# Left output rows in an accumulator of their own, and memory rows transposed by 128 columns, in a recurrent-memory attention kernel

## The chip, the cores and the metric

The kernel runs on one core of a Trainium2 chip. The metric is the device time of one execution in microseconds (us). The kernel before was timed three times: median 1837.84 us, from 1831.92 to 1839.93. Besides, one execution was taken by the hardware profiler.

## The reference

The output is the sum of three terms over x of 2048 tokens by 1024: x itself, a memory-augmented attention over the normalised x, and a feed-forward block with tanh-GELU on the same. The attention goes through the tokens in 64 segments of 32, one after the other, because each takes eight memory rows from the one before:

```
for s in range(n_seg):                       # 64 segments of 32 tokens
    h = concatenate([mem, xs])               # 8 memory rows + 32 tokens
    q, k, v = h @ Wq, h @ Wk, h @ Wv         # 32 heads of 128
    p = softmax(where(mask, q k^T * scale, -1e9))
    o = (p v) @ Wo
    mem = o[:8]; outs.append(o[8:])          # the memory rows feed the next segment
```

Weights are bfloat16, 1024 x 4096 for each of Wq, Wk, Wv and 4096 x 1024 for Wo: 32 MB in all, more than fits on the core.

## The kernel before

*Stages.* Until about 450 us the kernel does the layer norm and the feed-forward block (lines 304 to 643). Its result with x added, R, is kept in DRAM (`R_n`) and laid out anew for the recurrence by `turn_R` (L433): as rows of the main tokens in `hr_d` and of the left tokens in `hrL_d`. From then on come the 64 segments.

*Main and left rows.* A segment's own pass has only 32 rows: 24 tokens and 8 memory rows. The last 8 tokens of each segment, called left, are put together for four segments (32 rows) and have their Q, K, V and output made at a later time. Which is made in which segment goes by the kind of the segment, `i4 = s % 4` (L730 to L733): left K first half in kind 3 and second in kind 0, left Q first half in kind 1 and second in kind 2, left V first in kind 0 and second in kind 3, and the left output in kind 1 (and in the last segment). `og` and `slot` number the group and the place in it.

*Weights.* They are cut into 64 units of 128 x 2048: 8 for each of six half passes in the order K0, Q0, K1, Q1, V0, V1, and 16 for the output pass, O. 46 stay in SBUF. 18 are streamed anew in each segment through a ring of six buffers: SP issues the load of the next one as soon as PE has used up a buffer (`unit_done`, `start_stream`). In O, units 3, 6, 8, 11, 14 and 15 are streamed. Two of the 18 are kept in PSUM and copied to the ring by VectorE (DVE) at L245, two copies of 128 x 512 words each; the one that is unit 4 of Q0 is copied right after the first unit of K0. One more is kept in SBUF by five eighths.

*One product.* PE's array is used in four column strips of 32. A unit's `product` (L738) is four matmuls of 128 x 32 weights (the activations, loaded) by 512 columns, one for each strip. Products of left rows use the same unit with other activations (`hL`) into an accumulator of their own. There are three accumulators in PSUM (`acc`), one bank for scores and small things (`mixed`), and four with kept weights.

*The output pass* (L1109 to L1123). `o_product(n, t, acc)` multiplies unit n, two heads. In kinds 0, 2 and 3 the first nine units put even and odd heads into different strips, so that after unit 9 `fold` (L1001) adds the two halves on ScalarE (ACT) and DVE, and the other seven go to a second accumulator. In kind 1 main and left rows go through one accumulator of 64 columns' width in two halves, with no fold. `values(1, ...)` (L926), the attention's second half of heads, is made inside this pass after unit 5; its results are copied out of PSUM by ACT and DVE and are the weights of units 8 to 15.

*The turn* (L1124 to L1161). The new memory rows have to reach the next segment's `hT`, the transposed input. They are copied or added out of the accumulator to `o_sb` (by ACT at L1130 in kind 1, by DVE with the folded half at L1134 in the others), `put_mem` (L286) transposes them with matmuls against unit columns, and DVE casts them into `hr_home` (L297). Up to six left products of the next segment are "led" (`lead_products`, L753): three ahead of `put_mem` and three after it. Then the residual R is added (L1154) and the rows are stored: in kinds 0, 2, 3 by four DMAs on POOL (L1188); in kind 1 by four DMAs (two on ACT, two on POOL, L1160) to `outL_d` in DRAM, and from there to the output (L1185).

*Queues.* ACT, DVE, POOL and SP work in the order of the program. POOL carries the load of the next segment's x and R (`hr_home`, L267), the load of the left residual (`pd_main`, L1121), most stores, and in segments 1 to 5 the `small` DMAs of `turn_R`, which are put in one or two at a time after streamed units. The order of all work is written out by hand; the framework adds the waits.

Of the kernel before, what the change touches and what calls it, by code (L numbers as in the profile page):

```python
# [17 lines left out]
P = 128  # L18
S = 2048
DM = 1024  # L20
# [36 lines left out]
AT_BANKS, AT_PART = 5, 4  # L57
PART_COLS = 1280
# [31 lines left out]
def kernel(  # L90
# [37 lines left out]
    outL_d = dram.tile([NGRP, 2 * SEG, DM], BF16, name="outL_d")  # L128
# [157 lines left out]
    def put_mem(o_sb, hT, ps, nb=4):  # L286
# [4 lines left out]
        for c in range(nc_):  # L291
            for q in range(4):
                nc.tensor.matmul(  # L293
                    psM[32 * q:32 * q + 32, c, :, :], lhsT=o_sb[:, 4 * c + q, :], rhs=rows,
                    start=(c == 0), stop=True, skip_group_check=True, tile_position=(0, 32 * q),
                )
# [7 lines left out]
    with tc.tile_pool(name="ma", bufs=2) as ma, tc.tile_pool(name="mps", bufs=6, space=PSUM) as mps:  # L304
# [124 lines left out]
        def with_left(seg):  # L429

            return seg % GRP == 1 or seg == NSEG - 1

        def turn_R(ttg, eng, small=None):  # L433
# [3 lines left out]
            for i in range(4):  # L437
# [3 lines left out]
                both = [  # L441
                    t[:, 256:512].rearrange("(h r) c -> r h c", h=2)
                    for t in (hr_d[min(4 * og + 1, NSEG - 1) + 1, :, :], hrL_d[og, :, :])
                ]
                halves = [rows.rearrange("t (h w) c -> t w h c", w=2)[:, w, :, :] for w in range(2)]
                if with_left(seg):
                    m0 = SEG
                    pairs = [(both[w][m0:m0 + SEG, :, :], halves[w]) for w in range(2)]
                else:
                    pairs = [(hr_d[seg + 1, :, 256:512].rearrange("(j t) c -> t j c", j=4), rows)]  # L450
# [5 lines left out]
                for r0 in rows_at:  # L456
                    pairs += [(both[w][r0:r0 + NL, :, :], halves[w][NX:SEG, :, :]) for w in range(2)]
# [62 lines left out]
        for tg in range(4):  # L520
# [88 lines left out]
            else:  # L609
# [4 lines left out]
                put_mem(o_sb, nxt["hT"], mps.tile([P, 512], F32, name="ps"))  # L614
# [35 lines left out]
    with tc.tile_pool(name="late", bufs=1) as late, \  # L650
# [69 lines left out]
        for s in range(NSEG):  # L720
# [14 lines left out]
            m0 = SEG if left_o else main_row(slot)  # L735
            st = {}

# [188 lines left out]
            def values(u, rs):  # L926
# [18 lines left out]
                for r in rs:  # L945
# [4 lines left out]
                    else:  # L950
                        parts = [
                            ((outL if u else outs0)[:, h, NL * slot:NL * slot + NL], 0, NL),
                            (outM[:, h, :] if u else outs0[:, h, m0:m0 + SEG], NL, 40),
# [17 lines left out]
            def o_product(n, t, acc):  # L971
# [3 lines left out]
                w, i, u = unit  # L975
                for k in range(2):
                    h = 4 * (i % 4) + 2 * u + k
                    main = outM[:, h, :] if i >= 4 else outs0[:, h, m0:m0 + SEG]
                    if left_o:
                        lhs = [(0, 32, outL[:, h, :]), (32, 32, main)] if i >= 4 else [(0, 64, outs0[:, h, :])]  # L980
                        tiles = [(64 * r + r0, w, (2 * r, 2 * r + 1), lhsT) for r0, w, lhsT in lhs for r in range(2)]
                        start, stop = n == 0 and k == 0, n == 15 and k == 1
                    elif n < NPAIR:
                        tiles = [(64 * k + 32 * r, 32, (r, r + 2), main) for r in range(2)]
                        start, stop = n == 0, n == NPAIR - 1
                    else:
                        tiles = [(32 * r, 32, (r,), main) for r in range(4)]
                        start, stop = n == NPAIR and k == 0, n == 15 and k == 1
# [116 lines left out]
            at = {5: [lambda: values(1, (0, 1))]}  # L1105
# [3 lines left out]
            psX = new_acc()  # L1109
            for n, unit in enumerate(O_UNITS):  # L1110
                t = unit_tile(unit)
                if n == NPAIR and not left_o:
                    st["folded"] = fold(psX)
                    psX = new_acc()
                o_product(n, t, psX)
                unit_done(unit)
                for fn in at.get(n, ()):
                    fn()
                if n == 6 and left_o:
# [4 lines left out]
            nw = 2 if left_o else 1  # L1124
            if not final:
                o_sb = outM
                no = 16 if left_o else 8
                o = psX[:, 0:32 * no].rearrange("p (h e) -> p h e", e=32)
# [97 lines left out]
```

## Time and profile before

| | |
|---|---|
| median of three runs | 1837.84 us |
| the profiled execution | 1834.89 us |
| its span, first to last instruction | 1833.2 us |
| granted TensorE clock | 0.998 |
| PE busy / DVE / ACT / POOL | 94% / 52% / 36% / 15% |
| DRAM traffic over the span | 336 GB/s |
| first segment begins at | 363.5 us |
| a group of four segments, 605 to 1740 us | 85.2 to 88.6 us |

On the profile's page each digit of a row is the busy share of one of 40 equal slices, in tenths. A group's line names the source line, the engine, the operation, what is written and read, shapes, count, then busy time, mean length of one, and the idle time ahead with what ended it. A window's row gives the length, busy time and count for PE, PE's weight loads, DVE, ACT and POOL, the granted clock, and the share and rate of the 16 DMA engines. Matmuls overlap, so that four of 380 ns in four strips start within some 10 ns and the next four 215 ns later. The landing of SP's own transfers is not in the trace.

### The profile page before, as it was taken

The numbers are of one execution on the slowest core, as the hardware profiler recorded it, in microseconds if no ns is written. First come the engines' busy times: TensorE is split into PE (matmuls) and PEld (weight loads), VectorE is DVE, ScalarE is ACT, GpSimd is POOL, SyncE is SP. The second block draws the span as 40 slices with busy tenths as digits, with TensorE's granted clock in tenths as the row PEclk, the third lists the DMA queues.
The fourth block names the chain that finished last, engine by engine and source line by source line (L and its number), as shares of the span: only waits on it lengthen the run. The fifth ranks groups of instructions, "written<-read, shape, count | busy, mean of one in ns | idle before, by whom it ended". The sixth has DMA issues, their size and how long they took to land.

```text
span 1833.2 us, 71272 instructions
## 1 busy us (share of the span) xinstructions
PE 1720.8 (94%) x31117; PEld 872.6 (48%) x31137; DVE 962.2 (52%) x2444; ACT 665.4 (36%) x1509; POOL 276.4 (15%) x542
## 2 busy tenths in 40 slices
PE   8999999998998999999999999999999999999997
PEld 4444444444444444554445545444445444444444
DVE  7657483805554545545455555555555454545543
ACT  6334251602333333333333334333333333333333
POOL 0000001500342111112111111111111111111111
PEclk9999999999999999999999999999999999999999
DMA  9921212769999999999999999999999999999997
GB/s 291 319 85 46 55 44 57 261 209 367 400 398 365 383 389 390 380 385 380 376 382 389 393 385 386 389 387 391 374 389 383 373 393 383 381 380 390 378 386 301
DMA packets 230821, 604.65 MB, mean 330 GB/s; under 512 B 46795, under 2 KB 86267, under 8 KB 230508
## 3 DMA queue, kind: packets, MB, share of 16 engines
q1 hardware_dynamic: 207252, 579.67, 83.6%
q0 software_dynamic: 16384, 16.64, 2.9%
q8 instruction: 244, 4.00, 0.9%
q10 hardware_dynamic: 6872, 3.78, 0.7%
q14 instruction: 69, 0.57, 0.1%
HBM read 586.02 MB, written 29.10 MB: 336 GB/s over the span
## 4 chain that ended last, share of the span: by engine, by line
PE 42%; DMA 22%; issue 3%; DVE 2%; ACT 1%; DVEq 0%; ACTq 0%; SPq 0%; POOLq 0%
PE acc L744 29%; DMA u<-Wc_V 10%; PE acc L991 9%; DMA u<-Wc_O 7%; DMA u<-Wc_Q 2%; DMA u<-Wc_K 2%; PE acc L934 1%; DVE d_oL L1012 1%; DVE u L245 1%; DMA hr_home<-hr_d 1%; PE mixed L853 1%; ACT mixed L897 1%; PE mixed L293 1%; PE mixed L859 0%; ACT q_all L1130 0%
## 5 line engine op out<-in xcount | busy, mean ns | idle before, releaser
L744 PE MATMUL acc<-u,hr_home 128*32 128x512 bf16 x11520 | 790.3, 380 | 43.7 <-DMA u<-Wc_V 17.5
L744 PEld LDWEIGHTS <-hr_home 128*32 128x32 bf16 x12288 | 334.1, 96 | 352.0 <-issue 60.2
L744 PE MATMUL acc<-u,hrL 128*32 128x512 bf16 x2880 | 247.2, 379 | 2.1 <-issue 1.0
L473 PE MATMUL ps<-u 128*128 128x512 bf16 (+1 forms) x920 | 194.4, 373 | 2.0 <-ACT u L390 2.0
L245 DVE TENSOR_SCALAR u<-kept 128x512 uint32<-128x512 uint32 x254 | 163.6, 686 | 62.0 <-PE acc L991 41.6
L795 ACT CAST d_oL<-acc 128x512 bf16<-128x512 f32 x128 | 74.6, 583 | 275.0 <-PE acc L744 275.0
L991 PE MATMUL acc<-u,q_all 128*32 128x256 bf16 (+1 forms) x2207 | 133.8, 300 | 20.0 <-DMA u<-Wc_O 15.0
L594 PE MATMUL ps<-u 128*128 128x512 bf16 x657 | 146.2, 379 | 0.8
L473 PEld LDWEIGHTS <-u 128*128 128x128 bf16 x920 | 89.8, 98 | 104.9 <-issue 2.4
L1188 POOL DMA_DIRECT2D out_dram<-hr_home x188 | 96.3, 513 | 260.8 <-DVE hr_home L1154 247.0
L991 PE MATMUL acc<-u,d_oL 128*32 128x512 bf16 (+1 forms) x1536 | 131.6, 382 | 1.2 <-DMA u<-Wc_O 0.7
L907 DVE TENSOR_TENSOR pd_main<-half_home,mixed 128x320 bf16<-128x320 bf16 x128 | 62.4, 488 | 132.2 <-ACT mixed L897 132.2
L809 DVE STREAM_TRANSPOSE q_all<-q_all 128x512 bf16<-128x512 bf16 x128 | 90.6, 708 | 71.1 <-ACT q_all L795 71.0
L991 PEld LDWEIGHTS <-q_all 128*32 128x32 bf16 x3381 | 99.8, 96 | 58.9 <-issue 27.9
L799 ACT CAST q_all<-acc 128x512 bf16<-128x512 f32 x128 | 75.2, 587 | 139.1 <-PE mixed L859 138.7
L267 POOL DMA_DIRECT2D hr_home<-hr_d x58 | 32.8, 565 | 591.0 <-PE acc L744 572.6
L744 PEld LDWEIGHTS <-hrL 128*32 128x32 bf16 x3072 | 84.9, 96 | 51.3 <-issue 7.6
L795 ACT CAST q_all<-acc 128x512 bf16<-128x512 f32 x128 | 75.2, 587 | 93.5 <-PE acc L744 93.5
L594 PEld LDWEIGHTS <-u 128*128 128x128 bf16 x672 | 65.3, 98 | 77.3 <-DVE g_u L555 0.4
L897 ACT ACTIVATE mixed<-mixed,small_consts 128x160 f32<-128x160 f32 x256 | 94.3, 368 | 8.4
L547 ACT ACTIVATE g_xb<-ps,b1col 128x512 bf16<-128x512 f32 x112 | 76.8, 686 | 55.5 <-PE ps L473 54.7
L991 PEld LDWEIGHTS <-d_oL 128*32 128x32 bf16 (+1 forms) x2048 | 65.5, 99 | 59.1 <-issue 12.2
(137 smaller groups left out, 2104.6 us busy)
## 6 DMA issues: line engine op xcount, KB each, us to landing
u<-Wc_K SPq DMA_DIRECT2D x256, 512.0 KB
u<-Wc_V SPq DMA_DIRECT2D x256, 512.0 KB
u<-Wc_O SPq DMA_DIRECT2D x256, 512.0 KB
u<-Wc_Q SPq DMA_DIRECT2D x192, 512.0 KB
u<-in_B_w_dram SPq DMA_DIRECT2D x28, 512.0 KB
u<-Wc_O SPq DMA_DIRECT2D x64, 192.0 KB
hr_home<-hr_d POOLq DMA_DIRECT2D x58, 128.0 KB, 5.3
u<-in_A_Wq_dram SPq DMA_DIRECT2D x13, 512.0 KB
```

What stands on the lines that cost most here:

```text
L245: nc.vector.tensor_single_scalar(out=out, in_=in_, scalar=0, op=ALU.bitwise_or)
L473: nc.tensor.matmul(ps[:, SEG * s0:SEG * s1].rearrange("p (s t) -> p s t", t=SEG), lhsT=w1_sb[fb // 2][:, kt, (fb % 2) * P:(fb % 2 + 1) * P ...
L547: nc.scalar.activation(out=xb[:, :], in_=ps[:, :], func=ACT.Identity, bias=b1col[:, fb:fb + 1], scale=1.0)
L594: nc.tensor.matmul(ps[:, :], lhsT=gts[fc // 4][:, fc % 4, t * P:(t + 1) * P], rhs=w2_sb[fc // 2][:, fc % 2, cs], start=(fc == 0), stop=(fc ...
L744: nc.tensor.matmul(o, lhsT=lhs[:, i, :], rhs=m, start=(i == seq[0]), stop=(i == seq[-1]), tile_position=(0, 32 * j),)
L795: cp(out=out, in_=ps.rearrange("p (h e) -> p h e", e=32))
L799: cp(out=t[:, :], in_=ps[:, :])
L809: nc.vector.transpose(out=home, in_=home)
L897: nc.scalar.activation(out=mixed[:, 160 * b:160 * b + 160], in_=mixed[:, 0:160], func=ACT.Exp, scale=-1.0, bias=off[:, b:b + 1],)
L907: nc.vector.tensor_tensor(out=pdA.rearrange("p c b q -> p b c q"), in0=prA[:, None, :, :].to_broadcast([P, 2, 4, 40]), in1=dd, op=ALU.mult,)
L991: nc.tensor.matmul(acc[r0:r0 + rows, c:c + wide], lhsT=lhsT, skip_group_check=True, rhs=cols, start=start, stop=stop, tile_position=(0, r0),)
L1188: nc.gpsimd.dma_start(out=out_flat[rows, 256 * j:256 * j + 256], in_=res[32 * j:32 * j + NX, :])
```

## The change

Lines of the kernel after are shown with +.

1. `put_mem` takes four heads at once as 128 columns: two matmuls where there were 8 (16 in kind 1). Only the very first call keeps the old form.
2. In kind 1 (and the last segment) the main rows go through O as in the other kinds, with the fold after unit 12. The left rows get an accumulator of their own, `psL`: for ten units their product follows the main one, and for units 0, 1, 2, 4, 5 and 7 it is put off: three ahead of `put_mem` and three after it.
3. In kind 1 no left Q products are led; the second left Q half is made wholly in the pass Q1 of kind 2.
4. `values(1)` in kind 1 is made in two halves, after unit 5 and after unit 7; the first eight heads' results go to `pr_all`. The left residual's load comes after unit 7 in place of 6.
5. Main rows of kind 1 are stored straight from `hr_home`, as in the other kinds. The left rows are added to their residual in four steps and stored by one DMA on ACT; `outL_d` and the residual rows in `hrL_d` have a layout by four column blocks, so that `turn_R` needs one DMA for a piece of left rows where it took two.

```diff
+LEFT_LATER, LEFT_PAIR = (0, 1, 2, 4, 5, 7), 12
...
-    def put_mem(o_sb, hT, ps, nb=4):
+    def put_mem(o_sb, hT, ps, nb=4, wide=True):
...
         for c in range(nc_):
+            if wide:
+                nc.tensor.matmul(
+                    psM[:, c, :, :], lhsT=o_sb[:, 4 * c:4 * c + 4, :].rearrange("p h e -> p (h e)"), rhs=rows,
+                    start=(c == 0), stop=True, skip_group_check=True,
+                )
+                continue
             for q in range(4):
...
-                if with_left(seg):
-                    m0 = SEG
-                    pairs = [(both[w][m0:m0 + SEG, :, :], halves[w]) for w in range(2)]
-                else:
-                    pairs = [(hr_d[seg + 1, :, 256:512].rearrange("(j t) c -> t j c", j=4), rows)]
+                pairs = [(hr_d[seg + 1, :, 256:512].rearrange("(j t) c -> t j c", j=4), rows)]
...
-                for r0 in rows_at:
-                    pairs += [(both[w][r0:r0 + NL, :, :], halves[w][NX:SEG, :, :]) for w in range(2)]
+                left = hrL_d[og, :, 256:512].rearrange("(j t) c -> t j c", j=4)
+                pairs += [(left[r0:r0 + NL, :, :], rows[NX:SEG, :, :]) for r0 in rows_at]
...
-            m0 = SEG if left_o else main_row(slot)
+            m0 = main_row(slot)
+            low_outs = pr_all.rearrange("p (h t) -> p h t", h=8) if left_o else outM[:, 0:8, :]
...
+            def o_product(n, t, acc, left=0):
+                pairs = LEFT_PAIR if left_o else NPAIR
                 for k in range(2):
                     h = 4 * (i % 4) + 2 * u + k
+                    if left:
+                        lhs = outL[:, h, :] if i >= 4 else outs0[:, h, 0:SEG]
+                        tiles = [(64 * k + 32 * r, 32, (r, r + 2), lhs) for r in range(2)]
+                        start, stop = left == 1, left == 16
...
-            at = {5: [lambda: values(1, (0, 1))]}
+            if left_o:
+                at = {5: [lambda: values(1, (0,))], 7: [lambda: values(1, (1,))]}
+            else:
+                at = {5: [lambda: values(1, (0, 1))]}
...
+            def left_product(n, t):
+                nonlocal left_made, psL
+                if psL is None:
+                    psL = new_acc()
+                left_made += 1
+                o_product(n, t, psL, left_made)
+
             for n, unit in enumerate(O_UNITS):
                 t = unit_tile(unit)
-                if n == NPAIR and not left_o:
+                if n == (LEFT_PAIR if left_o else NPAIR):
                     st["folded"] = fold(psX)
                     psX = new_acc()
                 o_product(n, t, psX)
+                if left_o and n in LEFT_LATER:
+                    left_later.append((n, t))
+                elif left_o:
+                    left_product(n, t)
                 unit_done(unit)
...
-                if left_o:
-                    nc.scalar.copy(out=o_sb[:, 0:no, :], in_=o)
...
-                if (i4 == 3 or more) and not final:
+                if i4 != 1 and (i4 == 3 or more):
...
                     lead_products(LEAD // 2)
-                put_mem(o_sb, nxt["hT"], mixed[:, 224:288], 4 // nw)
+                for _ in range(len(left_later) // 2):
+                    left_product(*left_later.popleft())
+                put_mem(o_sb, nxt["hT"], mixed[:, 224:288])
                 if led:
                     lead_products(LEAD)
+            while left_later:
+                left_product(*left_later.popleft())
...
+            nc.vector.tensor_tensor(out=res, in0=flat, in1=res, op=ALU.add)
+            if left_o:
+                resL = st["resL"]
+                for k in range(2):
+                    for b in range(2):
+                        q = slice(64 * b, 64 * b + 64)
+                        nc.vector.tensor_tensor(
+                            out=resL[q, :], in0=psL[64 * k:64 * k + 64, 256 * b:256 * b + 256], in1=resL[q, :],
+                            op=ALU.add,
+                        )
+                let_go(psL)
+                if not final:
+                    nc.scalar.dma_start(out=outL_d[og, :, :], in_=resL)
```

## The prediction

> **What bounds the kernel now.** I read the page first (parts 1 to 3), then windows over single stages, then the waits of TensorE, then the timeline of one turn. All sums are made against the profiled execution, 1834.89 us (span 1833.2), which stands 2.95 us below the median of the runs, 1837.84.
>
> The page's busy shares, DMA row and first queue:
>
> ```profile
> span 1833.2 us, 71272 instructions
> ...
> PE 1720.8 (94%) x31117; PEld 872.6 (48%) x31137; DVE 962.2 (52%) x2444; ACT 665.4 (36%) x1509; POOL 276.4 (15%) x542
> ...
> DMA  9921212769999999999999999999999999999997
> ...
> q1 hardware_dynamic: 207252, 579.67, 83.6%
> ```
>
> PE looks like the bound at 94%, but from slice 11 on the 16 DMA engines are at 9 as well, nearly all of it the weight stream of queue q1. Windows over the end of segment 25 and the start of 26 (columns: us, busy time by engine, clock, DMA share, GB/s) tell where each leads:
>
> ```profile
> 990.45:994.45 4.00, 4.00 (x52) 1.94 (x48) 1.24 (x4) 1.98 (x6) 0.96 (x2) 1.00 1.03 404
> 994.45:997.00 2.55, 2.55 (x50) 1.34 (x52) 1.29 (x2) 0.00 (x0) 0.16 (x1) 1.00 1.04 398
> 997.00:1000.00 3.00, 2.91 (x74) 1.39 (x66) 0.45 (x2) 0.58 (x1) 0.00 (x0) 1.00 0.84 315
> 1000.00:1003.00 3.00, 3.00 (x64) 1.52 (x56) 2.54 (x6) 0.58 (x1) 1.12 (x2) 1.00 1.02 357
> 1003.00:1010.00 7.00, 7.00 (x200) 3.99 (x192) 4.18 (x13) 3.19 (x8) 2.44 (x5) 1.00 1.03 396
> ```
>
> A share of 1.03 is DMA at its limit; only about the turn of a kind-1 segment it falls to 0.84. There the six stream buffers are full and SP waits for PE. From the 13 groups of four segments at 605 to 1740 us: mean 87.26 us, DMA share 1.003. At 1.03 the same traffic takes 87.26 x 1.003 / 1.03 = 85.0 us, so 2.3 us of each group is lost DMA time. Over the same four-microsecond stretch (6 to 10 us after the output pass begins) the 13 windows average a share of 0.86, that is 0.68 us lost, and with its two neighbours 0.9 us.
>
> A rule that speaks the other way: the Trainium skill (Perfetto Trace Analysis, Roofline) puts the ceiling of a core's 16 DMA engines at about 435 GB/s. A group moves 385 GB/s x 87.26 us = 33.6 MB, by the rule 77 us: ten us of slack, PE alone the bound, and earlier buffers worth nothing. The rows never exceed 410 GB/s where the share is 1.03, so I take 85.0. The groups themselves agree: summing PE's gaps over 150 ns by what ended them, those not ended by a DMA range from 0.95 to 4.16 us a group, and the group's length doesn't follow them (correlation -0.01; beside the group's DMA time as second variable, 0.24 us per us). PE stalls are paid out of PE's own waits for the stream, 2.4 us a group:
>
> ```profile
> PE acc L744 <- DMA u<-Wc_V: 17.5, 38, 1.8
> PE acc L991 <- DMA u<-Wc_O: 15.8, 33, 1.5
> ```
>
> **The change part by part.** Times are from the start of the output pass (O) of a kind-1 segment, 990.45 in segment 25. Before, O takes 16 units of 0.43 us: attention values at 2.71, last product over at 7.5, first K product of the next segment at 9.17, the same in 10 of 16 such segments.
>
> *O pass.* Six left products (each 4 matmuls, 0.215 us) leave: -1.29. But `values(1)` now comes after six units that take 5 x 0.215 + 0.43 = 1.5 us, while its probabilities (L912) end at 1.76 to 1.87: kinds 0 and 2, whose O is already single, finish it at 2.12. I take 2.05 for its first half, a stall of about 0.35. In two halves, each with the same 0.245 us (both row tiles ran side by side), it costs +0.25, and the second half needs the first's bank, which ACT empties 0.72 us after the first half (2.77): +0.1 with the drain. Then eight units of 0.44: O ends at 6.75, **0.75 earlier**. `fold` at unit 12 has four double units (1.7 us) against 2.05 that it takes in single segments; three left products (0.645) cover the rest.
>
> *Turn.* The timeline before:
>
> ```profile
> 998.23 0.58 ACT L1130 CAST q_all<-acc 128x512 bf16<-128x512 f32 x1 [4.10 <-PE acc L991]
> 998.86 0.27 PE L293 MATMUL mixed<-ident_mem,q_all 128*32 128x16 bf16 x16
> 999.21 0.23 DVE L297 CAST hr_home<-mixed 128x64 bf16<-128x64 f32 x1 [2.76 <-PE mixed L293]
> 999.62 0.39 PE L744 MATMUL acc<-u,hr_home 128*32 128x512 bf16 x4
> 999.78 0.42 DVE L1154 TENSOR_TENSOR pd_main<-acc,pd_main 128x256 bf16<-128x256 f32 x1 [0.34 <-DMA pd_main<-hrL_d]
> 1000.12 0.42 DVE L1154 TENSOR_TENSOR hr_home<-acc,hr_home 128x256 bf16<-128x256 f32 x1
> 1000.45 1.28 DVE L245 TENSOR_SCALAR u<-kept 128x512 uint32<-128x512 uint32 x2
> ```
>
> Six products fill it before and after (led Q before, left output after), ACT's 0.58 becomes DVE's add of 0.42, over at 7.47; memory product 7.53 to 7.70 (below), three left products, K begins at 8.34, **0.83 earlier**.
>
> *What is late next.* DVE's queue: after the memory copy and the residual add stand now four adds of 64 partitions (0.34 apart, the last two waiting on the first two) in place of two, behind the landing of the left residual, and behind them the two copies L245 that PE needs at its 13th product (Q unit 4). The residual's DMA is issued at 3.78 (3.60 before; it follows the values), and lands a median of 4.9 us later:
>
> ```profile
> DMA to landing us min/median/max: 2.5/4.9/5.8
> ```
>
> With 5.1 (the mean of the steady ones): adds from 8.98, copies from 10.45 to 11.73. PE reaches that product at 8.34 + 2.59 = 10.93: **a new stall of 0.85**, which eats K's lead. ACT's store of the left rows waits for the same adds, and ACT's copy of K behind it; DVE's transpose comes later still, so it adds nothing.
>
> *Second Q pass of kind 2.* Six more products, +1.29; the 0.28 that PE waits there for `keep_q` (L883 on L245) goes. Sum for PE in a group: -0.83 + 0.85 + 1.29 - 0.28 = **+1.03**. The waits for the stream hide it: at 0.24 it is +0.25 a group, in 15 groups +3.7 (with that cover gone, +15).
>
> *DMA.* O's six streamed units and the first three of the next segment give their buffers back 0.65 to 0.85 earlier, exactly where DMA is idle (0.9 to be had): -0.7 a group, **-10.5**. Traffic: 128 packets of 512 B less into `outL_d`, main rows straight from SBUF, left rows in smaller packets; at 27 ns for 512 B and 46 for 1024, over 16 engines, 0.13 us a group: -2.
>
> *Memory rows by 128 columns*, all 64 turns. The 8 matmuls took 0.064 us of PE (16: 0.114). Phase A's 128-column loads stand 0.056 apart, so two take 0.11. The Trainium skill (TensorEngine Tiling, Tiling Modes) says that a change of tiling mode drains the array, and these are the only 128x128 ones here. The row agrees:
>
> ```profile
> 993.40 0.18 PE L940 MATMUL acc<-q_all,VL 64*128 64x32 bf16 x2
> ...
> 993.51 0.62 PE L991 MATMUL acc<-u,d_oL 128*64 128x512 bf16 x4
> ```
>
> 0.10 from one mode to the other. So 0.17, +0.1 a turn by the rule, +0.05 without; I take 0.1, in full at the 16 turns after kind 3 (PE leads there, DMA at 0.88 to 0.95), at 0.24 at 32 others: +2.4. If no transition cost shows it is half.
>
> *Start.* Turning R into rows takes one DMA in place of two for each left piece: 34 on POOL in segments 1 to 4 in place of 57. Before, that backlog reaches segment 5:
>
> ```profile
> 550.06 2.08 POOL L1188 DMA_DIRECT2D out_dram<-hr_home  x4 [3.23 <-issue]
> 558.02 0.58 POOL L267 DMA_DIRECT2D hr_home<-hr_d  x1 [5.88 <-PE acc L991]
> ```
>
> Segment 4's stores go out at 550, 13 us into segment 5, and the load of x behind them lands 6 us late; segment 5 takes 26.4 us against 23. The stream catches up a part: -2.5. *End*: 1.29 of left products and four adds after the last output, partly beside the first add: +0.5.
>
> Sum: -10.5 + 3.7 - 2 + 2.4 - 2.5 + 0.5 = **-8.4 us**; 1837.84 - 8.4 = 1829.4.
>
> **Rivals.** *DMA binds wholly* (0.20): PE's additions vanish in its waits, and the rows' 0.24 is noise. For it: the zero correlation. Against: four of 13 groups have under 1.5 us of DMA waits. -10.5 - 2 - 2.5 + 1.6 (the turns after kind 3): 1824.
>
> *The earlier buffers win nothing* (0.16): the six products merely change places with the led ones, the turn still gives no buffer back for 1.7 us (1.9 before), and the hole moves along. Then -2 - 2.5 + 2.4 + 0.5: 1836. For it: the hole lies in the turn, not in O. Against: in the steady trace it has a left edge, 6 us into O, where the backlog ends.
>
> *Slower* (0.20): the left residual lands late because DMA is now full in that window. Place: DVE's adds ahead of L245, in kinds 1 to 2. Each us of landing beyond 5.1 is one more us of PE stall; the 2.4 us of waits that pay for it are gone when it reaches 5.1 + 2.4 - 1.03 = 6.5, and the gain is used up near 7. At 8 us: +1.5 x 15 over the cover, less 10: **1850**. For it: loads of x at full DMA reach 6.8. Against: the longest of this one is 5.8.
>
> **How the numbers follow.** The likeliest case (0.44) gives 1829.4, with its own range 1821 to 1838 from: gain on DMA 0.45 to 0.9 a group (7 us), PE counted at 0 to 0.5 (7 us), 128-column turns 0.05 to 0.15. 0.5%, 9.2 us, is about what a measurement of this kernel can tell from no change (the three runs span 8). Faster by over 0.5%: a half of the likeliest and all of the first rival, 0.42; within: the other half and the third, 0.38; slower 0.20. The range 1817 to 1846 leaves out a part of the slow case and the fast tail.
>
> **What would show it.** O's span in kind 1 falls from 7.5 to 6.75 with a PE wait ahead of the values; DMA share at 6 to 10 us rises from 0.86 towards 0.95; PE waits at L744 on DVE's copy in the second segment of each group, 0.85; PE's waits for the stream shrink below 2.4 a group; segment 5 is 23 us. Wrong if the share in the hole stays, or if PE's waits for DVE exceed 2 us a group.

## The result, and the profile after

The changed kernel takes 1842.8 us (median of 20 runs, 1836.4 to 1850.7) against 1836.4 us for the kernel before (20 runs, 1828.5 to 1843.2). The ratio is 1.0033 with a 95% interval of 1.0019 to 1.0046: slower by 6 us, where 8.4 us faster was forecast. 1842.8 lies inside the range of 1817 to 1846; the direction was wrong.

The page of the changed kernel, whose profiled span is 1838.7 us:

```profile
span 1838.7 us, 71935 instructions
...
PE 1728.9 (94%) x31410; PEld 891.5 (48%) x31430; DVE 1005.5 (55%) x2545; ACT 668.1 (36%) x1526; POOL 264.0 (14%) x515
...
q1 hardware_dynamic: 206852, 579.66, 83.8%
```

PE is busy for 8 us more. The windows over the same stretches of segment 25 and 26 as before, counted from the start of the output pass (columns: us, busy time by engine, clock, DMA share, GB/s):

```profile
992.67:996.67 4.00, 3.87 (x76) 1.90 (x72) 1.25 (x5) 2.02 (x6) 0.71 (x2) 1.00 1.03 404
996.67:999.22 2.55, 2.55 (x69) 1.75 (x65) 1.96 (x4) 0.74 (x2) 0.41 (x1) 1.00 1.04 404
999.22:1002.22 3.00, 3.00 (x62) 1.43 (x58) 1.78 (x6) 0.00 (x0) 0.81 (x2) 1.00 0.98 363
1002.22:1005.22 3.00, 2.15 (x44) 0.99 (x36) 2.88 (x6) 0.58 (x1) 1.23 (x3) 1.00 1.01 350
1005.22:1012.22 7.00, 7.00 (x171) 4.19 (x164) 3.35 (x12) 2.96 (x7) 2.21 (x4) 1.00 1.01 390
```

The third row is the hole that the change was to close: its DMA share went from 0.84 to 0.98. Over the same stretch of all 13 groups (6 to 10 us into the output pass) the mean share rose from 0.86 to 0.95. The fourth has the new stall: PE is busy for 2.15 of 3.00 us. The timeline of that turn (start, length, engine, line, then the idle time ahead and what ended it):

```profile
1001.47 1.78 DVE L1170 TENSOR_TENSOR pd_main<-acc,pd_main 64x256 bf16<-64x256 f32 x4 [0.51 <-PE acc L739]
1003.28 1.29 DVE L246 TENSOR_SCALAR u<-kept 128x512 uint32<-128x512 uint32 x2
```

```profile
1002.09 1.68 PE L739 MATMUL acc<-u,hr_home 128*32 128x512 bf16 x28
1004.62 0.61 PE L739 MATMUL acc<-u,hr_home 128*32 128x512 bf16 x8 [0.85 <-DVE u L246]
```

The first K product starts at 1001.01, 8.34 us into O as forecast (8.34 to 8.36 in five of the 13 groups; in the others a wait inside O makes it later, median 8.59 against 9.17 before). DVE makes the four left sums, then the two copies of kept weights, and PE waits 0.85 us for them. Over the whole kernel, the waits of PE (us in total, times, longest):

```profile
PE acc L739 <- DVE u L246: 15.0, 16, 1.4
PE acc L739 <- issue: 10.9, 16, 1.9
PE acc L739 <- DMA u<-Wc_V: 10.5, 24, 1.8
...
PE acc L990 <- DMA u<-Wc_O: 7.2, 15, 1.2
```

The waits for the stream shrank (`Wc_V` 17.5 to 10.5, `Wc_O` 15.8 to 7.2), and 15 us of waits for DVE came. Mean lengths of a segment over the 13 groups from segment 8 to 59:

| us | kind 0 | kind 1 | kind 2 | kind 3 | group |
|---|---|---|---|---|---|
| before | 21.76 | 23.10 | 20.76 | 21.64 | 87.26 |
| after | 21.73 | 22.32 | 21.73 | 21.73 | 87.51 |

Kind 1 gained 0.78 us and kind 2 lost 0.97. What DMA won in kind 1 it lost in kind 2: its mean rate went from 386 to 396 GB/s in kind 1 and from 381 to 368 in kind 2. The same stretch late in kind 2, 12 to 16 us after segment 26 begins, kernel before and then after:

```profile
1011.43:1015.43 4.00, 2.89 (x63) 1.47 (x67) 0.74 (x3) 1.57 (x5) 0.56 (x1) 1.00 1.03 411
```

```profile
1012.68:1016.68 4.00, 4.00 (x120) 2.08 (x108) 2.09 (x6) 2.52 (x7) 0.58 (x1) 1.00 0.95 337
```

Before, PE had time to spare there (2.89 of 4.00) and the DMA share was 1.03; after, PE has none and DMA falls to 0.95 (means over 13 groups: 1.03 before, 0.97 after). The share over whole groups stayed at 1.003.

### The profile page after: what moved, and what is told of

Same layout as the page of the kernel before. It is cut to its first block, busy times and chain, and to the rows that moved or that the text cites. A ratio compares the mean times of both kernels' runs of the same rounds, so it can differ in the third digit from the quotient of the medians.

```text
span 1838.7 us, 71935 instructions
## 1 busy us (share of the span) xinstructions
PE 1728.9 (94%) x31410; PEld 891.5 (48%) x31430; DVE 1005.5 (55%) x2545; ACT 668.1 (36%) x1526; POOL 264.0 (14%) x515
## 4 chain that ended last, share of the span: by engine, by line
PE 59%; DMA 23%; issue 10%; DVE 5%; POOL 1%; ACT 1%; SPq 0%; DVEq 0%; ACTq 0%; POOLq 0%
PE acc L739 30%; DMA u<-Wc_V 8%; PE ps L467 8%; PE ps L588 8%; PE acc L990 8%; DMA u<-Wc_K 4%; DMA u<-Wc_O 4%; DMA pd_main<-hrL_d 2%; DMA u<-Wc_Q 2%; PE acc L929 2%; DMA hr_home<-hr_d 2%; DVE u L246 2%; DVE pd_main L1170 1%; ACT mixed L892 1%; DVE d_oL L1011 1%
## 5 line engine op out<-in xcount | busy, mean ns | idle before, releaser
L739 PE MATMUL acc<-u,hr_home 128*32 128x512 bf16 x11520 | 802.6, 380 | 49.1 <-DVE u L246 15.0
L739 PE MATMUL acc<-u,hrL 128*32 128x512 bf16 x2880 | 259.3, 380 | 2.1 <-issue 1.7
L246 DVE TENSOR_SCALAR u<-kept 128x512 uint32<-128x512 uint32 x254 | 163.5, 685 | 43.4 <-PE acc L990 18.4
L1193 POOL DMA_DIRECT2D out_dram<-hr_home x252 | 128.8, 514 | 320.0 <-DVE hr_home L1164 315.4
L990 PE MATMUL acc<-u,d_oL 128*32 128x512 bf16 x1944 | 138.9, 381 | 7.5 <-issue 4.8
L268 POOL DMA_DIRECT2D hr_home<-hr_d x58 | 33.0, 569 | 608.0 <-PE acc L739 603.6
L990 PE MATMUL acc<-u,q_all 128*32 128x256 bf16 (+1 forms) x2292 | 110.0, 283 | 8.8 <-DMA u<-Wc_O 4.3
L990 PEld LDWEIGHTS <-q_all 128*32 128x32 bf16 x3364 | 88.2, 96 | 56.5 <-ACT q_all L951 23.8
L990 PEld LDWEIGHTS <-d_oL 128*32 128x32 bf16 x2592 | 65.3, 96 | 57.4 <-issue 14.0
```

What stands on the lines that cost most here:

```text
L246: nc.vector.tensor_single_scalar(out=out, in_=in_, scalar=0, op=ALU.bitwise_or)
L739: nc.tensor.matmul(o, lhsT=lhs[:, i, :], rhs=m, start=(i == seq[0]), stop=(i == seq[-1]), tile_position=(0, 32 * j),)
L990: nc.tensor.matmul(acc[r0:r0 + rows, c:c + wide], lhsT=lhsT, skip_group_check=True, rhs=cols, start=start, stop=stop, tile_position=(0, r0),)
L1193: nc.gpsimd.dma_start(out=out_flat[rows, 256 * j:256 * j + 256], in_=res[32 * j:32 * j + NX, :])
```

## The experiments

All ratios are to the kernel before, timed in turn with it on the same chip; e1 to e4, e5 to e8, e9 to e11 and e12 to e14 were timed at four different times and on three chips, so kernels of different rounds are compared by their ratios alone. To compare the kernels, one number is taken from each profile: **TensorE's need**, the length of a group less those of its waits over 150 ns that a DMA ended (mean of 13 groups). "Issue" and "other" are the waits over 150 ns for which the profile shows no cause, and those that another engine ended; both are part of the need. Each profile is of one execution, so these columns have errors that the ratios don't have: from the scatter of the 13 groups, 0.2 to 0.5 us for a need and 0.2 to 0.4 for the issue waits. (e11, whose values were wrong, is left out here.)

| kernel | ratio, 95% interval | group | need | DMA waits | issue | other |
|---|---|---|---|---|---|---|
| before | 1 | 87.26 | 84.89 | 2.37 | 1.65 | 0.98 |
| changed | 1.0033 (1.0019 to 1.0046) | 87.51 | 86.23 | 1.28 | 1.47 | 1.97 |
| e1, rows by 32 | 1.0065 (1.0041 to 1.0090) | 88.21 | 86.93 | 1.28 | 2.31 | 2.19 |
| e2, rows by 128 alone | 0.9978 (0.9963 to 0.9993) | 87.07 | 84.23 | 2.84 | 1.20 | 0.63 |
| e3, copies first | 1.0051 (1.0033 to 1.0069) | 88.14 | 86.60 | 1.54 | 1.61 | 1.92 |
| e4, six more products | 1.0057 (1.0038 to 1.0075) | 88.73 | 86.75 | 1.98 | 2.07 | 1.01 |
| e5, left sums later | 1.0050 (1.0032 to 1.0069) | 87.54 | 86.38 | 1.16 | 1.57 | 2.02 |
| e6, memory rows four times | 1.0208 (1.0183 to 1.0233) | 89.57 | 88.23 | 1.34 | 3.84 | 0.91 |
| e7, bank alone | 1.0038 (1.0018 to 1.0057) | 87.74 | 85.82 | 1.92 | 1.70 | 1.14 |
| e8, moved and led | 1.0074 (1.0058 to 1.0091) | 87.86 | 86.00 | 1.86 | 1.69 | 1.21 |
| e9, stores last too | 0.9985 (0.9966 to 1.0004) | 87.17 | 85.89 | 1.28 | 1.91 | 1.20 |
| e10, narrow output tiles | 0.9996 (0.9978 to 1.0015) | 87.03 | 84.68 | 2.35 | 1.57 | 0.66 |
| e12, values in halves | 0.9990 (0.9970 to 1.0011) | 87.37 | 84.91 | 2.46 | 1.52 | 0.70 |
| e13, bank with late sums | 1.0104 (1.0069 to 1.0139) | 89.07 | 86.80 | 2.27 | 1.73 | 2.28 |
| e14, stores last alone | 1.0004 (0.9979 to 1.0028) | 87.35 | 85.98 | 1.37 | 1.40 | 1.99 |

**The memory rows.** e1 takes the 128-column form out of the changed kernel, e2 puts it alone into the kernel before.

```
e1, of the changed kernel, every turn:
-                put_mem(o_sb, nxt["hT"], mixed[:, 224:288])
+                put_mem(o_sb, nxt["hT"], mixed[:, 224:288], wide=False)
e2, of the kernel before:
-    def put_mem(o_sb, hT, ps, nb=4):
+    def put_mem(o_sb, hT, ps, nb=4, wide=True):
     ...
+            if wide:
+                nc.tensor.matmul(psM[:, c, :, :], lhsT=o_sb[:, 4 * c:4 * c + 4, :]..., rhs=rows, ...)
+                continue
```

> The changed kernel with the memory rows turned in 8 matmuls of 32 columns again; all else stays. In the changed kernel's trace PE's time from the first memory matmul to the next product is 0.144 us (0.064 before), so 0.08 us a turn, 64 turns, 5.1 us in all if nothing hides it. Theory A (PE time in the second half of each group is no longer covered by waits for the stream; the left bank and its adds are the loss): half of it at most, 1840 to 1843 against 1842.8, ratio to the kernel before 1.001 to 1.003. Theory B (the 128-column turn is the whole loss): the kernel before, ratio 0.999 to 1.001.

> The kernel before with the memory rows turned by 128 columns, and nothing else of the change. PE time +0.08 us at 48 turns, and in kind 1 four matmuls for 16, about +0.1. Theory A: +0.25 to 0.5 of it, +1 to +3 us, ratio 1.0005 to 1.0015. Theory B: the change's own ratio, 1.003.

e1 is slower than the changed kernel (1.0065 against 1.0033) and e2 faster than the one before (0.9978): the 128-column form is a gain of some 4 to 6 us in both surroundings, with errors of 3 to 5 us. From the first memory matmul to the next product it takes PE 0.144 us in place of 0.064; but a group of e2 has 60 PE instructions fewer than one of the kernel before (3595 against 3655), and its waits marked "issue" are 1.20 us in place of 1.65. Between e1 and the changed kernel they are 2.31 and 1.47. Both differences go the same way; neither alone is far outside its error.

**One price measured by itself.** e4 gives the kernel before the six products that the change put into the second Q pass of kind 2, as repeats of its first product, which change no result.

```
+                        for _ in range(EXTRA if n == 0 and (w, u) == ("Q", 1) and i4 == 2 and s > 4 else 0):
+                            product(w, n, tiles[n], hT, ps, [n])
```

> The kernel before with PE work added at the place where the change adds it: in the second Q pass of kind 2 the first unit's product is made six times more (each time from the start, so that the result stays), +1.29 us of PE in each of 15 groups, 19.4 us in all. It measures the price of PE time there. The prediction's 0.24: +4.7 us, ratio 1.0025. If it is covered wholly: 1.000. If the ring of stream buffers fills up meanwhile and DMA stands still (theory A): 0.5 to 0.9, +10 to +17 us, ratio 1.005 to 1.009.

1.0057 is 10.5 us for 15 x 1.29 = 19.4 us of products: 0.54 us per us (0.36 to 0.71 over the interval), and not 0.24. The products also bring 48 PE instructions a group, and the issue waits of its profile are 2.07 us against 1.65, so a part of this price may be theirs.

**The stall at the copies.** e3, e5 and e9 put the four left sums behind the two copies of kept weights; they differ in where the left rows are stored.

```
-            if left_o:
-                resL = st["resL"]
-                for k in range(2): ... tensor_tensor(out=resL[q, :], ...)      # at the turn
+            half_pass("K", 0, left_k[0], {0: [left_at.pop()]} if left_at else {})  # after the first K product
 e3: outL_d stored on POOL, small stores queued there
 e5: outL_d stored on ACT after the K pass, small stores queued then
 e9: as e5, small stores queued in the output pass of kind 2, behind the load of x
```

> The changed kernel with the four adds of the left residual, and the store of the left rows, put after the first unit of the next segment, so that on DVE the two copies of the kept weights come ahead of them; the store goes out on POOL. The PE wait for the copies (0.61 to 1.3 us in each group, mean about 0.95) goes, all else stays. Theory A: most of it is won back, 0.5 to 0.95 us a group, 8 to 15 us, ratio 0.995 to 0.999. Theory C (PE stalls there are covered by waits for the stream, as the prediction has it, at 0.24): -3.5 us, ratio 1.0015. Theory B: no change, 1.003.

> The changed kernel, but the four adds of the left residual come after the first K product of kind 2, so behind the two copies of kept weights on DVE, and the store of the left rows (with the small stores behind it) goes out on ACT after the first K pass, not on POOL as in the run with the copies first. Nothing is left out. A sum used for this and the next runs: what TensorE needs of a group is its length less its waits for the stream; over the six kernels so far (before 84.89, changed 86.23, rows by 128 alone 84.23, rows by 32 86.93, copies first 86.60, six more products 86.75 us) the group's length follows it at about 0.5 us per us. Theory A (TensorE's need is what is paid, at that slope): the stall of 0.93 us a group at the copies goes, need 85.3, length 87.1, 0.4 us shorter in 15 groups, and the stall of segment 2: -7 us against the changed kernel, 0.9995 of before (0.998 to 1.001), kind 2 at 21.0 us. Theory B (DMA full in kind 2 sets the end, and TensorE's stall is paid by its waits for the stream): as the changed kernel, 1.003, kind 2 at 21.7, with the 0.93 coming back as waits for DMA.

> As the run with the left sums later, but the small stores of the left rows wait one pass more: they are queued on POOL behind the load of the next segment's x in kind 2, not ahead of it. Nothing is left out. In that run and in the one with the copies first, POOL's load of x in kind 2 began 2.2 us after the V pass and not 0.5, when the last small store ahead of it had landed, and TensorE waited 1.0 us a group for the memory rows at the turn of kind 2. If that is what gave the stall back: load of x 0.5 us after V again, kind 2 at 21.2 us or less, need of TensorE 85.3 us, ratio to before 0.999 (0.997 to 1.001). If the stall at the copies was paid by the stream anyway: 1.003 to 1.005 as in both runs before, whatever the load does.

In e3 and e5 the stall at the copies went, and another came, at the next turn. The waits of e5:

```profile
PE acc L740 <- DVE hr_home L304: 16.1, 14, 2.4
PE acc L740 <- DMA u<-Wc_V: 9.7, 23, 1.8
```

The first row is K0 of kind 3 waiting for the memory rows, whose cast waits for the tile into which x is loaded. The store on ACT did not cure it, so the store on POOL was not the reason. POOL's timeline of e5 shows more:

```profile
916.36 2.30 POOL L1193 DMA_DIRECT2D out_dram<-outL_d  x4 [7.53 <-DMA outL_d<-pd_main]
922.64 0.58 POOL L268 DMA_DIRECT2D hr_home<-hr_d  x1 [3.98 <-PE acc L991]
929.71 1.60 POOL L1212 DMA_DIRECT2D out_dram<-hr_home  x3 [6.48 <-DVE hr_home L1167]
```

The load of x (L268) stands behind four small stores and starts 3.98 us after the last of them was issued; on average it starts 2.0 us after the end of the V pass, where the kernel before has 0.5. It lands 5.0 to 6.6 us later, too late for the turn. The profile names PE as the releaser in 12 of 13 groups; but in all 13 groups of e5, and in the 13 of e3, the load starts 0.33 to 0.34 us after the second of the four stores has landed. It waits for that landing, though none of the semaphores that it waits for belongs to one of these stores. In e9 the stores stand behind the load:

```profile
1006.97 0.56 POOL L268 DMA_DIRECT2D hr_home<-hr_d  x1 [11.49 <-PE acc L740]
1007.59 1.21 POOL L1119 DMA_DIRECT2D out_dram<-outL_d  x2
1013.30 1.08 POOL L1119 DMA_DIRECT2D out_dram<-outL_d  x2 [4.50 <-issue]
```

The load starts 0.4 us after V, and now it is the third store that waits: in all 13 groups it starts 0.33 us after the load has landed. Both stalls are gone; what is left of the wait for the memory rows is

```profile
PE acc L740 <- DVE hr_home L304: 0.8, 3, 0.3
```

The time is 0.9985: 9 us below the changed kernel, with all its other parts kept.

e14 moves the small stores alone and leaves the sums where the change has them:

```
-                    small.append(...)                       # at the turn
+                left_small.append((og, left_rows))           # into small in O of kind 2, behind the load of x
```

> The changed kernel, with the small stores of the left rows queued behind the load of x in kind 2, and the left sums where the change has them, ahead of the kept copies. Nothing is left out. If the stall at the copies (0.93 us a group) is what the change pays: it stays, and the time is the changed kernel's, 1.003 (1.001 to 1.005), 9 us above the form with the sums moved too. If the stores ahead of the load were the cost: 0.9985.

The stall stays,

```profile
PE acc L740 <- DVE u L246: 18.3, 16, 2.9
```

and the time comes out at 1.0004 (0.9979 to 1.0028), between the two and distinct from neither: how the 9 us divide between sums and stores isn't settled.

**The moved products.** e7 keeps the bank, but moves no product and leads the second left Q again; e8 moves and leads.

```
e7: -LEFT_LATER, LEFT_PAIR = (0, 1, 2, 4, 5, 7), 12
    +LEFT_LATER, LEFT_PAIR = (), 12
e7, e8:
    -                if i4 != 1 and (i4 == 3 or more):
    +                if i4 == 3 or more:
e13: e7's edits on top of e9
```

> The changed kernel, but no left product is moved to the turn and the second left Q products are led again: the left rows' own bank, the layout of stores and the memory rows by 128 columns stay. Nothing is left out. O of kind 1 then ends about 1.3 us later than in the changed kernel, K0 begins near 9.3 us, and the copies of kept weights (done at 11.7) are in time for its 13th product at 11.9: no stall there. Theory A (TensorE's need is what is paid, earlier buffers win nothing): need 86.23 - 0.93 = 85.3, length 87.1, 0.9995 of before (0.998 to 1.001), 6 us faster than the changed kernel. Theory C (the earlier end of O was worth its 0.7 us of DMA a group and something else ate it): slower than the changed kernel, over 1.005. Kinds under A: 23.1, 20.8 for kinds 1 and 2.

> The changed kernel with the second left Q products led again, while the six left products stay at the turn: the turn now has twelve products. Nothing is left out. O ends as in the changed kernel (6.9), K0 begins 1.3 us later than there (near 9.6). Theory A: need 85.3 as in the run with the bank alone, the same time as that within 2 us, 0.9995 of before. Theory C (the earlier end of O gives DMA back 0.7 us a group): 10 us faster than the bank alone, 0.994. If the hole of DMA only moves into the longer turn: DMA share of 0.85 in it, and the time of the bank alone.

> The best form so far of the changed kernel (left sums behind the kept copies, small stores behind the load of x, 0.9985 of before), with no left product moved to the turn and the second left Q products led again, as in the run with the bank alone (1.0038). Nothing is left out. Both have the same work; only where O ends and K0 begins differs, 1.3 and about 1 us. If the moved products are worth what the prediction put on them (0.7 us of DMA a group, 10 us): 1.003 to 1.004, with waits of TensorE for the stream near 1.9 us a group and kind 1 at 23.4. If the late sums and stores made the whole difference: 0.9985, and the earlier end of O is worth nothing.

e7 has little of the stall (0.25 us a group) and was expected at 0.9995; it took 1.0038. Beside e2, which has the memory rows by 128 columns and nothing else of the change, that is 11 us more (6 to 16 over both intervals) for the bank, the values in halves, the four sums and the stores; of these only the halves and the number of instructions were tried alone (e12 and e10, below: 2 and 3 us, within their errors), so most of the bank's price stays open. e8, whose turn has twelve products so that K begins later, is slower still, though the hole closes in it as well (mean share 0.95): the earlier end of O alone is worth nothing here, and a gain was seen only where K came earlier too. Beside e9, e7 has the same need of TensorE (85.82 and 85.89) and takes 0.53% longer. That is 10 us, or 0.65 us a group (0.3 to 1.0 over both intervals), in favour of the moved products, close to the 0.7 that the prediction gave them; its DMA waits are 1.92 us a group against 1.28. The two differ in the late sums and stores as well. e13 was to show this with the same sums and stores on both sides, and did not: with leads in use, the late sums hold the third accumulator, and PE waits for it at the next pass.

```profile
PE acc L740 <- DVE pd_main L1184: 23.6, 15, 1.6
```

That is 1.6 us in each of 15 groups, all in kind 2. At 0.5 to 0.7 us per us it makes 12 to 17 us, and e13 is 12 us above e7.

**PE's instructions.** All 37 waits marked "issue" in the 13 groups of the kernel before ended between 1 and 2 us after a packet of queue q8 had landed; so did 38 of 38 in the changed kernel and 66 of 66 in e6. One such packet comes in about 6 us, so chance would put some six of 37 there. The packets are 16384 bytes and one comes for each 256 of PE's instructions: 3655 x 13 / 256 = 186, and 186 were there. So these are waits for PE's own program. e6 and e10 add instructions to the kernel before and to e2.

```
e6, of the kernel before:
-        for c in range(nc_):
+        for c in [c for _ in range(4) for c in range(nc_)]:
e10, of e2, first eight units of O in kind 1:
-  ... else [(0, 64, outs0[:, h, :])]
+  ... else [(0, 32, outs0[:, h, 0:32]), (32, 32, outs0[:, h, 32:64])]
```

> The kernel before, with the matmuls that turn the memory rows (32 columns) made four times over instead of once; same result, nothing left out. PE gets 3 x (48 x 0.064 + 16 x 0.114) = 14.7 us more work in all, and 240 more instructions a group. If only PE's time counts (0.5 us per us of it): +7 us, 1.004. If the number of PE's instructions has a price of its own beside their time (the run with rows by 128 columns has 60 fewer a group and is 4 us faster in spite of more PE time; solved together with the run of six more products: 0.33 us per us and 5 ns an instruction): 4.9 + 240 x 15 x 0.005 = +23 us, 1.0125, with TensorE's waits marked issue rising from 1.65 to over 2.5 us a group. Between them, 1.008, neither.

> The kernel before with memory rows by 128 columns (0.998 of before), and the first eight units of the output pass of kind 1 as two matmuls of 32 columns in place of one of 64. Nothing is left out, TensorE's time is the same (four tiles side by side in place of two, 0.43 us a unit), but a group has 64 more PE instructions, matmuls and weight loads, in 3.4 us of that pass; the changed kernel has 92 more there. All PE waits marked issue end 1 to 2 us after a 16 KB packet of the instruction queue (256 instructions of 64 B) has landed. If the number of instructions counts (9 ns each, by the run with the memory rows four times): +0.6 us a group of issue waits, most of it in kind 1 and the start of kind 2, of which a half to three quarters is paid: +5 to +7 us, 1.001. If only the time of the products counts: 0.998, issue waits at 1.2 us a group. It would then not be the instructions that make the own bank dear.

e6 took 37 us more, well over both forecasts. Its page and its waits of PE:

```profile
span 1868.9 us, 75132 instructions
...
q8 instruction: 259, 4.24, 0.9%
```

```profile
PE acc L744 <- issue: 35.4, 47, 2.0
PE acc L991 <- DMA u<-Wc_O: 11.9, 26, 1.0
```

The first of these rows in the kernel before:

```profile
PE acc L744 <- issue: 10.5, 15, 1.2
```

There are 15 more packets, and 35.4 us of waits at the products of K, Q and V, 10.5 before. In the 13 groups, 240 tiny instructions a group cost 2.2 us of waits beside about 1 us of PE time at the turns (the stretch from the first memory matmul to the next product went from 0.064 to 0.216 us, in kind 1 from 0.114 to 0.479). Only 10 of the 66 waits fall within 3 us of a turn (none of 37 before); the rest come later in the segments. In e10, 64 instructions that lengthen no product go with issue waits of 1.57 us where e2 has 1.20; its ratio lies 0.18% above e2's, and both differences are within their errors. So 240 more instructions a group have a price that is seen clearly. By the instruction it is 9 ns of waits in e6 and 6 in e10; whether it matters that they come in a burst is not shown.

**The values in halves.**

```
e11, e12, of e2:
+            at = {5: [lambda: values(1, (0,))], 7: [lambda: values(1, (1,))]} if left_o else ...
e12: -                if n == 6 and left_o:          # load of the left residual
     +                if n == 7 and left_o:
```

> The kernel before with memory rows by 128 columns, and the second attention values of kind 1 made in two halves, after units 5 and 7 as in the changed kernel, in place of both side by side after unit 5. Nothing is left out; no instruction more. TensorE's need rises by 0.25 us (halves one after the other) and up to 0.1 us a group: at 0.5, +2.6 us, ratio to before 0.9995, kind 1 at 23.3 us. If the halves also delay the fold or the later units (the second half of the heads' outputs comes 0.9 us later): over 1.002. The sum for the bank alone (1.0038) from 0.998: halves 2.6, instructions 5 to 7 us, the four adds and stores the rest, 1 to 3 us.

> The run with the values in halves again, but with the load of the left residual one unit later, behind the second half. In that run the load stood between the halves, into the buffer that the second half still reads, so that half of these values was made from the residual's bytes and TensorE waited for the load, 4.5 us a group over 150 ns, 105 us in all: its time says nothing of the halves. Here nothing is left out. Halves one after the other: +0.35 us of TensorE a group, 0.9995 of before against 0.998 for the rows by 128 alone; no cost: 0.998; over 1.002 if the later second half delays the fold or the last units.

e11's expectation overlooked the load of the left residual, which lands between the halves in the buffer that the second half reads: part of its values was made from other data, and 74.0 us of waits came of it.

```profile
PE acc L940 <- DMA pd_main<-hrL_d: 74.0, 17, 4.7
```

Its 1.0582 tells what one load costs that stands ahead of its buffer's last reader, nothing of the halves. e12 with the load behind them is 0.9990, against 0.9978 for e2: 2.2 us, near the 2.6 that was expected, with an error of some 5 us, so not told apart from nothing.

**All kernels together.** A fit made after the runs, over the 15 kernels of the table, of extra time per group ((ratio - 1) x 1836 / 15) on TensorE's need and on whether the six products are moved and not led:

```
extra us a group = 0.68 (+-0.06) x (need - 84.89) - 0.58 (+-0.13) if moved and not led
```

It leaves 0.2 us a group, 3 us of time; e4 is farthest off, 0.55 us a group below it. Whichever kernel is left out, the slope stays at 0.58 to 0.73 and the second number at 0.45 to 0.68. It is a relation between kernels that differ in several things, each need from one execution, and no proof of a cause by itself; e4 is the direct test of the price.

## Why the prediction was wrong, by its own steps

**Right in sum: what PE has to do.** K at 8.34, the stall of 0.85 (0.85 in segment 26, 0.93 on average) and the start of the sums (8.8 us into O, 8.98 put down) came as forecast. (The parts listed for O add up to -0.59 us, not to the -0.75 that was used; K's 8.34 bears out the second.) The sum was +1.03 us a group, and 4 x 0.1 for the memory rows: 1.43. The need rose by 86.23 - 84.89 = 1.34. Luck has a part in this: the memory rows took need away (0.66 us in e2, 0.70 between e1 and the changed kernel) where 0.4 was added for them, so the other parts added about 2.0 and not 1.03. With errors of 0.2 to 0.5 us in each need, where the rest comes from is open.

**About right: what DMA gains.** -0.7 us a group was forecast; e7 against e9 gives -0.65, the fit -0.58. The left edge of the hole was a true sign: over 13 groups its share rose from 0.86 to the 0.95 that was named. The rival by which earlier buffers win nothing falls with it, unless K is kept late (e8). The limit that the 0.7 was worked out with is less firm: it rests on rows that never exceed 410 GB/s, and other stretches of the same trace go to 422 over 4 us (919.45 to 923.45).

**The step that failed: "at 0.24 it is +0.25 a group, in 15 groups +3.7".** The waits for the stream do not hide PE's additions to that extent. Six products alone cost 0.54 us per us (e4), and over all kernels a us of need costs 0.68. So 1.34 x 0.68 = 0.91, less 0.58, is +0.33 us a group, **+5.0 us**; +6 was measured. In time, PE's additions with the memory rows were put at 3.7 + 2.4 = 6.1 us and cost 1.34 x 0.68 x 15 = 13.7: over half of the 14.4 us between forecast and result.

The trace shows where the cover ran out when it is split by the kind of segment (need, waits for the stream and length, means of 13):

| us | need before | after | stream waits before | after | length |
|---|---|---|---|---|---|
| kind 0 | 21.36 | 21.43 | 0.40 | 0.31 | -0.03 |
| kind 1 | 22.76 | 21.75 | 0.34 | 0.57 | -0.78 |
| kind 2 | 19.35 | 21.59 | 1.41 | 0.14 | +0.97 |
| kind 3 | 21.42 | 21.47 | 0.23 | 0.26 | +0.09 |

The stall and the six products both went into kind 2. It had the most cover of the four, 1.41 us, but the forecast itself put 0.85 + 1.29 - 0.28 = 1.86 there, and the need rose by 2.24. The waits gave 1.27 of it and the segment became 0.97 longer. In e4 the need of kind 2 rose by 1.43 and its length by 0.81. The prediction set all of PE's additions against one mean of 2.4 us a group.

The 0.24 was also weakly founded. It came from 13 groups of one execution; redone from the trace it is 0.25 with a standard error of 0.25, so those groups did not rule out 0.54 or 0.68. In the changed kernel, where kind 2 has no cover left, the group's length does follow the waits that no DMA ended: correlation 0.80, where the kernel before had -0.01. "DMA binds wholly" fails in the same way.

**Wrong sign: "+2.4" for the memory rows.** PE's time for them went up by 0.08 us a turn, where the prediction had 0.05 without and 0.1 with the drain at a change of mode that the Trainium skill states (TensorEngine Tiling, Tiling Modes); 0.08 lies between the two and does not tell. But e2 is 4 us faster. The step left out the instructions: 12 fewer at three turns of a group and 24 at that of kind 1, where e2 keeps four matmuls, make the 60. That they are the reason is likely, by e6, but not shown: e2's waits for other engines are lower too (0.63 us against 0.98).

**"-2.5" for the start.** Before and after alone speak against it: segment 5 falls from 26.4 to 23.6 us, but segment 6 rises from 19.9 to 22.1 and segment 2 from 20.8 to 23.6 (1.4 us of it are the stall at L246), so that segment 8 begins at 607.2 in place of 605.5. The other traces speak for it. From the start of segment 1 to that of segment 8 the six kernels with the old `turn_R` (before, e2, e4, e6, e10, e12) take 155.3 to 161.7 us, mean 158.5, and the kernel before is the shortest of them; the nine with the new one (changed, e1, e3, e5, e7, e8, e9, e13, e14) take 152.0 to 159.3, mean 154.6. Segment 5 has 25.6 to 27.9 us in the first and 21.4 to 23.6 in the second. So the backlog was worth about what was forecast or more. Traffic (33.58 to 33.49 MB a group) and end (0.4 us) came as forecast.

**The slower rival** had the place right, the queue of DVE ahead of L245, and the price wrong: it let the gain be used up at a landing near 7 us, and it was used up at the forecast landing (4.98 us on average in the 13 groups, 5.1 put down).

## What to carry to other kernels

In a stage where DMA and PE are both near their limits, neither hides the other: each us added to PE in every round cost 0.5 to 0.7 us here. A cover has to be counted in the stage where the work is put, not as a mean over the round, and a price that is read from the scatter of 13 groups needs its error beside it. Measure it with a few repeated products before relying on a cover. When work moves to an earlier time, look through the in-order queues for what must still come first (two copies, one load of x): here the late sums and the late stores together were worth 9 us, where the change had cost 6.

Two versions come out below both kernels: the kernel before with only the memory rows by 128 columns (0.9978), and the changed one with left sums behind the copies and stores behind the load of x (0.9985, interval up to 1.0004).

## What the runs showed of the hardware

In these kernels PE's waits without a visible cause are waits for its instructions. They always ended 1 to 2 us after a 16 KB packet of q8 landed (37 of 37 in the kernel before). Such a packet took 1.02 us there (median of 186), and the waits sum to 1.65 us a group: 25 us over 15 groups. More instructions bring more of them: 240 more a group, in tiny matmuls and their weight loads, made it 3.84 us.

A store issued on POOL can hold back a later load there until it has landed, and the profile can then name another releaser: in e5 PE, where in each of 13 groups the load followed the landing of the second store by 0.34 us. In e9, with the order turned round, the third store followed the landing of the load by 0.33 us, 13 times in 13. Why it is just that landing stays open.
